# Chunked retention with a running state, run between the FFN matmuls, in a retention + FFN kernel

## The chip, the cores and the metric

The kernel runs on one core of one Trainium2 chip. The metric is the time of one execution on the device in microseconds (us), given as the median of several runs. Each kernel is also profiled once; the span of that profile (first to last instruction) is 1.7 to 2.8 us shorter than the time of the same execution. Engines are named as in the profile: PE is the matmul engine, PEld its weight loads, DVE the vector engine, ACT the scalar engine, POOL the general engine, SP the queue that issues most DMAs. PE writes its results to PSUM banks: in the changed kernel a bank is a tile of 128x512 f32 (`hp`, `st`, `op` and so on), which another engine must read before it is written again. An eviction is the copy out of a bank; a cast is a copy from f32 to f16.

## The reference

Retention is attention without softmax: scores are multiplied by a decay that depends on the distance between the two tokens, and future tokens are dropped. The result, laid out as 4608 tokens of 512 features, goes through an FFN with a tanh-approximated Gelu.

```python
# q, k, v: [8 batches, 8 heads, 576 tokens, 64]
scores = scale * q @ k.T
gamma  = 1.0 - 2.0 ** (-5.0 - arange(H))
ret    = scores * where(rel >= 0, gamma ** rel, 0.0)     # rel = i - j
attn   = ret @ v
x      = attn.transpose(0, 2, 1, 3).reshape(4608, 512)
h      = x @ w_in                                        # 512 -> 2048
g      = 0.5 * h * (1 + tanh(c * (h + 0.044715 * h**3)))
out    = g @ w_out                                       # 2048 -> 512
```

The FFN is nine blocks of 512 tokens; each needs 64 "up" and 64 "down" matmuls of 128x128 weights and 512 columns. The retention of one batch depends on nothing outside it, and FFN block t needs no batch beyond t.

## The kernel before

There are two stages in series. Stage one goes through 32 pairs of heads. Each pair is loaded in pieces of 64 floats, transposed in f32 on PE, and the full causal triangle of scores is masked on DVE:

```python
for b in range(B):
    for hp in range(HP):
        ...                                   # [cut: loads, v cast]
        qT = do_transpose(q2, "qT", scale)    # f32 transposes, ACT eviction
        kT = do_transpose(k2, "kT", 1.0)
        for J in range(NJ):                   # every key chunk ...
            w = S - 128 * J                   # ... against all later queries
            for (x0, n) in chunks:
                for hl in range(2):           # the two heads of the pair
                    nc.tensor.matmul(st, kT[...], qT[...], start=True, stop=True)
                for hl in range(2):
                    nc.vector.tensor_tensor(out=rets[hl][...], in0=sts[hl][...],
                                            in1=G[...], op=ALU.mult)
        ...                                   # [cut: AV matmuls, ACT evictions]
        nc.gpsimd.dma_start(out=xT[hp, :, b * S : (b + 1) * S], in_=xst)  # x to DRAM
```

Stage two reads x back and evaluates the Gelu in four steps, two on ACT and two on DVE, with four PSUM banks for `hps`:

```python
for tb in range(NTB):
    ...                                       # [cut: load xr from DRAM]
    for fc in range(16):
        hps = mps1.tile([128, TB], F32, ...)  # 4 banks
        ...                                   # [cut: 4 matmuls]
        nc.scalar.activation(out=s1, in_=hps, func=AF.Square, scale=SQ_SCALE)
        nc.vector.scalar_tensor_tensor(out=u, in0=s1, scalar=C_G, in1=hps, ...)
        nc.scalar.activation(out=th, in_=u, func=AF.Tanh)
        nc.vector.scalar_tensor_tensor(out=gT[:, fc, :], in0=th, scalar=1.0, in1=hps, ...)
    for tcc in range(4):
        ...                                   # [cut: 16 matmuls, eviction x 0.5, store]
```

## Time and profile before

| | before |
|---|---|
| time, median of 3 runs (range) | 539.69 us (534.5 to 547.18) |
| span of the profile | 536.7 us |
| retention, until the first FFN matmul | 277.9 us |
| FFN, nine blocks of 28.06 us and the tail | 258.8 us |

The first lines are from the page of the profile: busy time of each engine, then the same in 40 equal slices of the span, in tenths (the clock line shows what share of full speed PE was granted).

```profile
PE 458.3 (85%) x2432; PEld 232.2 (43%) x2432; DVE 317.3 (59%) x673; ACT 283.9 (53%) x527; POOL 23.7 (4%) x47
...
PE   0275699888888888888759999999999999999997
...
PEclk9999999889889899898659999999999999999999
DMA  8869646778776776720020202021111212020202
```

The 85% of PE is an average of two stages. The table of stretches separates them: the columns are the stretch, its length, the busy time of PE, PEld, DVE, ACT and POOL with instruction counts, the granted clock, the DMA share and GB/s.

```profile
100.00:200.00 100.00, 85.42 (x587) 50.80 (x586) 65.55 (x180) 38.08 (x89) 8.10 (x15) 0.93 0.73 161
355.06:383.12 28.06, 27.78 (x129) 12.50 (x128) 19.74 (x33) 20.11 (x36) 0.00 (x0) 1.00 0.17 57
```

The second line is one FFN block. PE works 27.78 of 28.06 us, and DVE and ACT have 8 us to spare: this stage is bound by PE. In the first line, retention, no engine is full. The view of waits (engine, line, what it waited for, total us, times, longest) says that DVE waits for the scores and PE waits for the masks (30.1 of DVE's 106.8 us is a single wait, at the start of the run):

```profile
DVE ret L176 <- PE st L167: 106.8, 36, 30.1
...
PE st L167 <- DVE ret L176: 27.0, 90, 0.8
```

These are groups of instructions (busy us and mean ns of one, then idle time before them):

```profile
L176 DVE TENSOR_TENSOR ret<-st,G 128x320 f16<-128x320 f32 (+5 forms) x384 | 139.3, 425 | 128.0 <-PE st L167 106.8
L229 PE MATMUL hps<-xr,w_in_sb 128*128 128x512 f16 x576 | 144.2, 382 | 8.5 <-DMA xr<-xT 5.6
...
L246 DVE SCALAR_TENSOR_TENSOR gT<-th,hps 128x512 f16<-128x512 f32 x144 | 97.5, 680 | 1.6 <-ACT th L245 0.7
```

A matmul record is longer than the matmul's share of the engine, because matmuls overlap in the pipeline: 382 ns here, while the starts of FFN matmuls are 216 ns apart. For PE, spacing is the number to use.

### The profile page before, as it was taken

To read this page: it belongs to the slowest core of one execution; us is meant where nothing else is said; L and a number is where in the kernel's file an instruction comes from. 1 tells how busy PE (TensorE), PEld (TensorE's weight loads), DVE (VectorE), ACT (ScalarE), POOL (GpSimd) and SP (SyncE) were. 2 spreads that over 40 slices of the span, in tenths; PEclk is the share of its full clock that TensorE was granted. 3 is DMA by queue.
4 is the path that set the end of the run, shared out by engine and by line. 5 is a ranking of instruction groups with operands and counts; after the bars stand their busy time and mean duration, and the time that the engine had idled before them with its cause. 6 is when DMAs were issued, how large, how long until landed. Compare 5 with 4: busy or idle time off the path is not lost.

```text
span 536.7 us, 7161 instructions
## 1 busy us (share of the span) xinstructions
PE 458.3 (85%) x2432; PEld 232.2 (43%) x2432; DVE 317.3 (59%) x673; ACT 283.9 (53%) x527; POOL 23.7 (4%) x47
## 2 busy tenths in 40 slices
PE   0275699888888888888759999999999999999997
PEld 0132255555545555454424444444444444444443
DVE  0033337566666666666519495867768594939392
ACT  0843535334333333343118585867777676858583
POOL 0300001000000000000000000000000000000000
PEclk9999999889889899898659999999999999999999
DMA  8869646778776776720020202021111212020202
GB/s 331 175 237 236 153 102 152 179 177 177 155 156 145 156 163 137 154 67 22 24 89 1 98 21 98 21 78 39 58 61 40 79 40 78 25 94 2 78 1 79
DMA packets 129733, 56.06 MB, mean 104 GB/s; under 512 B 116896, under 2 KB 121504, under 8 KB 129184
## 3 DMA queue, kind: packets, MB, share of 16 engines
q1 hardware_dynamic: 89760, 41.44, 28.6%
q10 hardware_dynamic: 38400, 9.44, 8.1%
q0 software_dynamic: 1536, 4.72, 2.9%
q8 instruction: 19, 0.31, 0.2%
q14 instruction: 18, 0.15, 0.1%
HBM read 41.42 MB, written 14.16 MB: 104 GB/s over the span
## 4 chain that ended last, share of the span: by engine, by line
PE 49%; issue 34%; DMA 6%; ACT 4%; DVE 3%; POOL 2%; ACTq 1%; SPq 0%; POOLq 0%; DVEq 0%
PE ops L257 23%; PE hps L229 20%; DMA wtmp_o<-in_moe_w_out_dram 3%; POOL xT L207 2%; PE trps L137 2%; DMA vh<-in_v_dram 2%; PE avA L188 2%; PE st L167 1%; ACT w_in_sb L84 1%; DVE gT L246 1%; DVE ret L176 1%; ACT G L62 1%; DVE u L241 1%; DMA xr<-xT 1%; PE avB L197 1%
## 5 line engine op out<-in xcount | busy, mean ns | idle before, releaser
L176 DVE TENSOR_TENSOR ret<-st,G 128x320 f16<-128x320 f32 (+5 forms) x384 | 139.3, 425 | 128.0 <-PE st L167 106.8
L229 PE MATMUL hps<-xr,w_in_sb 128*128 128x512 f16 x576 | 144.2, 382 | 8.5 <-DMA xr<-xT 5.6
L257 PE MATMUL ops<-w_out_sb,gT 128*128 128x512 f16 x576 | 141.3, 379 | 0.0
L246 DVE SCALAR_TENSOR_TENSOR gT<-th,hps 128x512 f16<-128x512 f32 x144 | 97.5, 680 | 1.6 <-ACT th L245 0.7
L167 PE MATMUL st<-qT,kT 64*128 64x320 f16 (+5 forms) x384 | 73.6, 298 | 27.5 <-DVE ret L176 27.0
L245 ACT ACTIVATE th<-u 128x512 f32<-128x512 f32 x144 | 89.4, 624 | 3.6 <-DVE u L241 3.1
L229 PEld LDWEIGHTS <-w_in_sb 128*128 128x128 f16 x576 | 56.5, 98 | 79.2 <-issue 13.5
L257 PEld LDWEIGHTS <-gT 128*128 128x128 f16 x576 | 56.3, 98 | 68.0
L143 ACT ACTIVATE qT<-trps 128x576 f16<-128x576 f32 x32 | 20.8, 650 | 89.1 <-PE st L167 64.3
L188 PE MATMUL avA<-ret,vr 128*64 128x512 f16 (+3 forms) x256 | 61.9, 379 | 2.1 <-DVE ret L176 0.2
L205 ACT CAST xst<-avA 128x512 f16<-128x512 f32 x32 | 18.7, 585 | 58.2 <-PE avA L188 37.7
L167 PEld LDWEIGHTS <-kT 64*128 64x128 f16 (+1 forms) x384 | 26.5, 98 | 52.7 <-issue 42.4
L265 ACT ACTIVATE ost<-ops 128x512 f32<-128x512 f32 x36 | 20.5, 596 | 50.6 <-PE ops L257 50.6
L188 PEld LDWEIGHTS <-vr 128*64 128x64 f16 x256 | 30.2, 130 | 31.8 <-issue 19.1
L197 PE MATMUL avB<-ret,vr 128*64 128x64 f16 (+1 forms) x320 | 32.6, 221 | 0.0
L197 PEld LDWEIGHTS <-vr 128*64 128x64 f16 (+1 forms) x320 | 26.5, 132 | 4.4
L207 POOL DMA_DIRECT2D xT<-xst x32 | 17.4, 544 | 232.9 <-ACT xst L206 232.9
L143 ACT ACTIVATE kT<-trps 128x576 f16<-128x576 f32 x32 | 20.7, 645 | 6.2 <-PE trps L137 4.6
L130 ACT CAST vr<-vh 128x512 f16<-128x512 f32 x32 | 20.2, 630 | 0.0
L137 PE MATMUL trps<-ident,q_104 128*128 128x128 f32 (+1 forms) x5 | 1.4, 414 | 17.6 <-DMA q_104<-in_q_dram 17.5
L131 ACT CAST vr<-vh 64x128 f16<-64x128 f32 x32 | 9.5, 298 | 0.0
L130 ACT ACT_TABLE_LOAD x1 | 1.3, 1283 | 14.9 <-DMA vh<-in_v_dram 14.9
(428 smaller groups left out, 330.4 us busy)
## 6 DMA issues: line engine op xcount, KB each, us to landing
out_dram<-ost SPq DMA_DIRECT2D x36, 256.0 KB, 2.0
vh<-in_v_dram ACTq DMA_DIRECT2D x64, 128.0 KB, 3.5
xT<-xst POOLq DMA_DIRECT2D x32, 144.0 KB, 2.3
xr<-xT SPq DMA_DIRECT2D x36, 128.0 KB, 2.4
wtmp_i<-in_moe_w_in_dram SPq DMA_DIRECT2D x1, 4096.0 KB, 13.4
wtmp_o<-in_moe_w_out_dram SPq DMA_DIRECT2D x1, 4096.0 KB, 15.9
vh<-in_v_dram ACTq DMA_DIRECT2D x32, 32.0 KB, 3.6
q_104<-in_q_dram SPq DMA_DIRECT2D x2, 128.0 KB, 2.2
```

Source lines behind the costliest of these rows:

```text
L130: nc.scalar.copy(out=vr[:, 0 : NJ - 1, :, :], in_=vh[:, 0 : NJ - 1, :, :])
L143: nc.scalar.activation(out=tsb, in_=ps, func=AF.Copy, bias=0.0, scale=sc_mul)
L167: nc.tensor.matmul(st[0:njs, 0:n], kT[poff : poff + 64, 128 * J : 128 * J + njs], qT[poff : poff + 64, 128 * J + x0 : 128 * J + x0 + n], s ...
L176: nc.vector.tensor_tensor(out=rets[hl][0:njs, J, x0 : x0 + n], in0=sts[hl][0:njs, 0:n], in1=G[0:njs, h0 + hl, x0 : x0 + n], op=ALU.mult,)
L188: nc.tensor.matmul(avA[poff : poff + 64, 128 * J : 512], vr[0:128, J, hl, :], ret[0:128, J, 0 : 512 - 128 * J], start=(J == 0), stop=(J == 3),
L197: nc.tensor.matmul(avB[poff : poff + 64, 0 : S - 512], vr[0:njs, J, hl, :], ret[0:njs, J, 512 - 128 * J : S - 128 * J], start=(J == 0), st ...
L207: nc.gpsimd.dma_start(out=xT[hp, :, b * S : (b + 1) * S], in_=xst,)
L229: nc.tensor.matmul(hps, w_in_sb[:, ct, 128 * fc : 128 * fc + 128], xr[:, ct, :], start=(ct == 0), stop=(ct == 3),)
L245: nc.scalar.activation(out=th, in_=u, func=AF.Tanh, bias=0.0, scale=1.0)
L246: nc.vector.scalar_tensor_tensor(out=gT[:, fc, :], in0=th, scalar=1.0, in1=hps, op0=ALU.add, op1=ALU.mult,)
L257: nc.tensor.matmul(ops, gT[:, ft, 128 * tcc : 128 * tcc + 128], w_out_sb[:, ft, :], start=(ft == 0), stop=(ft == 15),)
L265: nc.scalar.mul(out=ost, in_=ops, mul=0.5)
```

## The change

The intent is fourfold. Retention is done in 128-token chunks: inside a chunk by masked scores, across chunks by a 64x64 state per head that is carried on, so the work grows linearly with the length. The decay is put into q and k when they are cast to f16, so one 0/1 mask serves all heads. x stays in SBUF. The Gelu becomes one activation. And the order of PE is fixed by hand, so that the retention of batch t+1 runs in ten steps between the matmuls of FFN block t.

The core of the diff (heavily cut):

```diff
-  G = const.tile([128, H, S], F32, name="G")               # decay table per head
+  cm = const.tile([128, NC, 128], F32, name="cm")           # 0/1 causal mask of a chunk
-  xT = dram.tile([HP, 128, NT], F16, name="xT")
+  xT = const.tile([128, HP, NT], F16, name="xT")            # SBUF
+  def ld():                                                 # one ring for all f32 loads
+      return sb.tile([128, 512], F32, tag="ld", name="ld", bufs=15)
   ... [cut: load_batch, cast_batch (q or k times the decay), weight loads and casts]
+  def score_pairs(b, pairs, tail):      # 128x128 scores of each chunk, x cm on DVE
+  def state_mm(b):                      # k^T v of each chunk, 64x64, 32 matmuls
+  def state_scan(b):                    # DVE: w = gamma^128 (w + u); ACT copies to tbd
+  def av_pairs(b, pairs, tail):         # ret @ v, then += q @ state; ACT copies to xT
+  def up(fc):
+      hp = bank("hp", 2, "hp")                              # 2 banks, 6 for the rest
+      ... [4 matmuls]
+      nc.scalar.activation(out=gT[:, fc, :], in_=hp, func=AF.Gelu_apprx_tanh)
+  slots = {1: 0, 2: 1, 3: 2, 5: 3, 7: 4, 8: 5, 11: 6, 14: 7, 16: 8, 19: 9}
+  with tc.manual_schedule(engines={PE}):
+      load_batch(0); cast_batch(0, ...); [load w_in]; load_batch(1)
+      for s in att_steps(0): s()
+      [cast w_in; load and cast w_out]
+      for t in range(NTB):
+          if t + 1 < B: cast_batch(t + 1, ...); steps = att_steps(t + 1)
+          if t + 2 < B: load_batch(t + 2)
+          for i, f in enumerate(ffn_steps(t)):              # 16 up + 8 down steps
+              f()
+              if i in slots and slots[i] < len(steps): steps[slots[i]]()
```

## The prediction

> **What bounds the kernel now.** There are two stages in series. By the table of stretches and the chain of waits, retention lasts until 278 us and the FFN from there to 536.7 us.
> - FFN: each 512-token block of 128 matmuls takes 28.06 us (three equal stretches), PE busy 27.8 of it: 219 ns per 128x512 matmul. Nine blocks make 252.5 us. PE-bound.
> - Retention: about 6.5 us per head pair in steady state (timeline), 32 pairs. No engine is full: in 100–200 us PE is busy 85%, DVE 66%, DMA 73%; PE waits on the DVE mask (128x512: 686 ns) and DVE on PE.
> - Start: nothing but the w_in load until 17.5 us, then two 7 us weight casts blocking ACT.
>
> **What the change does.**
> - Removes quadratic scores: per batch the masked score columns drop from 8x1600 to 8x512+2x256, the f32 transposes (about 110 ns each at their spacing, 320 of them) become 36 f16 ones per batch, and the xT round trip through DRAM goes.
> - The FFN loses Square, Tanh and both DVE steps (ACT 20 and DVE 20 of 28 us per block); one Gelu of about 0.59 us remains. PE still needs 28.06 us per block. "ScalarE: Activation LUTs" (The pipeline for one element) says that every function costs the same per element; the trace's Square and Tanh (0.59, 0.62 us) agree.
> - PE order is fixed by hand: 156 small matmuls per batch (36 transposes, 36 scores, 32 state, 52 AV) go between FFN matmuls of the previous block.
>
> **Costing.** "TensorE: Matmul & The Clock Gate" (Back-to-back issue gap) gives about 81 ns per weight-load-plus-matmul at N=128. This trace's 64-column AV group issues every 72 ns; scores in two row halves overlap. Estimate 65 ns: 156 x 65 = 10 us per batch, seven times = 70 us in blocks 0 to 6.
> Estimated from the trace's durations, DVE needs 16–18 us per block (masks, scan, evictions, casts), ACT about 18, Pool about 10: below 38, so blocks are PE-bound. But with two hp banks (four before), fill 0.88 + drain 0.2 + Gelu 0.59 us just fits two periods of 0.88: the state copies on ACT, waiting for the scan on DVE, hold Gelus up. I allow 2 us per block, 14 us.
> Start: 18 q/k/v DMAs at about 0.6 us issue each, Pool casts of q and v, cold batch-0 retention: PE reaches the FFN near 33 us; then batch 1, whose loads wait for load buffers freed by the w_in casts, stalls it to about 47 us.
>
> **Sum.** 47 + 252.5 − 1.8 (two up steps done) + 70 + 14 + 3.5 (last eviction and store) = 385 us.
>
> **Prediction: 385 us, 80% range 360 to 410; faster 0.98, same 0.01, slower 0.01.**
>
> **What would show it right or wrong.** FFN matmuls stay at 219 ns spacing; blocks 7 and 8 take about 28 us each and blocks 0 to 6 about 40. Small matmuls cost 50–90 ns at their spacing. PE over 90% busy after 50 us, clock 1.0. One idle gap of about 10 us on PE at 33–47 us, released by casts of batch 1. A few PE waits per block on Gelu.
>
> **What would make it wrong.** Small matmuls at 90+ ns, or full row/column overlap (40 ns): ±25 us. Pool casts two to three times slower than about 1 us, through sharing with DVE, would stall every block. In-order ACT or DVE queues holding Gelu for microseconds. A smaller start-up if batch 1 arrives early.

(On the page "ScalarE: Activation LUTs" the sentence on equal cost stands under "Step-by-step: what each stage is for", not under the section that the prediction names. In the result below the Gelu takes 0.598 us, as long as Square and Tanh.)

## The result, and the profile after

| | before | after |
|---|---|---|
| time, median of 4 runs | 539.4 us | 361.74 us (360.63 to 361.88) |
| first FFN matmul | 277.9 us | 35.1 us |
| FFN block with a batch of retention inside | – | 35.1 to 35.9 us |
| FFN block alone | 28.06 us | 27.6 us |
| span | 536.7 us | 358.8 us |

The ratio of the times is 0.671 (95% interval 0.667 to 0.675).

The same lines of the page:

```profile
PE 316.4 (88%) x2400; PEld 159.1 (44%) x2400; DVE 125.9 (35%) x269; ACT 161.9 (45%) x303; POOL 70.3 (20%) x101
...
PE   0176368799999999999999999999999999999995
...
PEclk9995669899999999999999999999999999999999
DMA  9979989994692898598937931100110011011012
```

From the ninth slice on PE is full, to the last but one. The loads that used to keep the DMA engines busy in the retention stage are now spread over the first 60% of the run. The table of stretches, for batch 0's retention, the gap after it, one combined block, and one block without retention:

```profile
18.00:35.10 17.10, 10.92 (x146) 7.82 (x144) 14.23 (x31) 8.78 (x19) 1.34 (x3) 0.78 0.92 282
35.10:48.40 13.30, 4.56 (x18) 1.77 (x17) 2.77 (x4) 3.92 (x6) 6.00 (x7) 0.63 1.12 211
157.50:192.60 35.10, 34.54 (x285) 17.57 (x284) 14.99 (x29) 17.32 (x33) 10.30 (x15) 1.00 0.76 168
327.20:354.80 27.60, 27.60 (x129) 12.42 (x127) 0.00 (x0) 11.90 (x20) 0.00 (x0) 1.00 0.10 38
```

In the third line PE is busy 34.5 of 35.1 us and DVE and ACT about half of it, so the block is bound by PE. In the second, PE is busy for only 4.6 of 13.3 us while the DMA share is at its limit (the view can show a share slightly over 1). The groups that answer to those of before, and the waits of PE:

```profile
L355 PE MATMUL hp<-xT,w_in_sb 128*128 128x512 f16 x576 | 141.6, 388 | 7.7 <-ACT gT L361 7.5
...
L361 ACT ACTIVATE gT<-hp 128x512 f16<-128x512 f32 x144 | 85.2, 598 | 58.6 <-PE hp L355 57.9
...
L246 DVE TENSOR_TENSOR ret<-st,cm 128x512 f16<-128x512 f32 x64 | 40.7, 684 | 49.5 <-PE st L221 49.4
...
L246 DVE TENSOR_TENSOR rett<-st,tm 128x256 f16<-128x256 f32 x16 | 6.1, 413 | 0.0
```

```profile
PE tr L189 <- DVE ck L146: 15.0, 4, 5.7
PE tr L189 <- POOL ck L146: 8.5, 3, 3.5
PE hp L355 <- ACT gT L361: 7.5, 14, 1.9
```

The mask on DVE fell from 139.3 to 46.8 us (40.7 for the full chunks and 6.1 for the tails of 64 tokens). PE's waits are now few: 15 us for batch 0's first casts, 8.5 us for batch 1's, and 7.5 us in all for a Gelu to free an `hp` bank.

The small matmuls are the part that the prediction mis-sized. From the timeline of PE (start us, length us, instruction):

```profile
163.89 0.62 PE L221 MATMUL st<-qk 64*128 64x128 f16 x16
164.44 0.69 PE L258 MATMUL us<-cv,ck 128*64 128x64 f16 x32
```

Sixteen score matmuls take 164.44 − 163.89 = 0.55 us, 35 ns each with the hand-over; the single records, which this view merges and which were read from the packed trace, start in twos 3 ns apart, one two every 55 to 56 ns. The 32 state matmuls take 20 ns each, and eight full-array transposes take 0.45 us, 56 ns each. Over the six combined blocks after block 0, the starts of the small matmuls add up to 37.3 us: 6.2 us per batch, 40 ns per matmul.

### The profile page after: what moved, and what is told of

Its sections match the earlier page's. It is cut to its first block, busy times and chain, and to the rows that moved or that the text cites. A ratio compares the mean times of both kernels' runs of the same rounds, so it can differ in the third digit from the quotient of the medians.

```text
span 358.8 us, 6008 instructions
## 1 busy us (share of the span) xinstructions
PE 316.4 (88%) x2400; PEld 159.1 (44%) x2400; DVE 125.9 (35%) x269; ACT 161.9 (45%) x303; POOL 70.3 (20%) x101
## 2 busy tenths in 40 slices
DMA packets 122715, 46.52 MB, mean 130 GB/s; under 512 B 113984, under 2 KB 113984, under 8 KB 122688
## 3 DMA queue, kind: packets, MB, share of 16 engines
q1 hardware_dynamic: 122688, 46.15, 55.2%
## 4 chain that ended last, share of the span: by engine, by line
PE 67%; ACT 10%; DMA 9%; DVE 7%; SPq 4%; issue 1%; POOL 1%; DVEq 0%; ACTq 0%
PE op L369 35%; PE hp L355 24%; DVE ret L246 4%; ACT gT L361 4%; SPq L118 3%; DMA ld<-in_moe_w_out_dram 3%; DMA ld<-in_q_dram 3%; ACT tbd_128 L281 2%; ACT tbd_130 L281 2%; PE xs L290 2%; DMA ld<-in_moe_w_in_dram 2%; PE xs L308 2%; PE st L221 2%; PE tr L189 2%; DVE ws L278 1%; DMA ld<-in_v_dram 1%
## 5 line engine op out<-in xcount | busy, mean ns | idle before, releaser
L355 PE MATMUL hp<-xT,w_in_sb 128*128 128x512 f16 x576 | 141.6, 388 | 7.7 <-ACT gT L361 7.5
L369 PE MATMUL op<-w_out_sb,gT 128*128 128x512 f16 x576 | 128.1, 379 | 0.0
L361 ACT ACTIVATE gT<-hp 128x512 f16<-128x512 f32 x144 | 85.2, 598 | 58.6 <-PE hp L355 57.9
L369 PEld LDWEIGHTS <-gT 128*128 128x128 f16 x576 | 55.6, 98 | 65.3
L377 ACT COPY ost<-op 128x512 f32<-128x512 f32 x36 | 21.1, 586 | 100.9 <-PE op L369 66.0
L246 DVE TENSOR_TENSOR ret<-st,cm 128x512 f16<-128x512 f32 x64 | 40.7, 684 | 49.5 <-PE st L221 49.4
L146 POOL TENSOR_TENSOR ck<-ld,sc 128x512 f16<-128x512 f32 (+1 forms) x35 | 34.8, 997 | 82.2 <-DMA ld<-in_k_dram 60.9
L195 DVE COPY qk<-tr 128x1024 f16<-128x1024 f16 x32 | 21.9, 686 | 56.5 <-PE tr L189 56.5
L146 DVE TENSOR_TENSOR cq<-ld,sc 128x512 f16<-128x512 f32 (+1 forms) x35 | 22.6, 660 | 40.2 <-DMA ld<-in_q_dram 40.2
L142 POOL CAST cv<-ld 128x512 f16<-128x512 f32 (+1 forms) x40 | 23.1, 590 | 67.4 <-DMA ld<-in_v_dram 36.8
L281 ACT CAST tbd_128<-ws 64x256 f16<-64x256 f32 x32 | 12.9, 403 | 3.1 <-DVE ws L278 2.6
L281 ACT CAST tbd_130<-ws 64x256 f16<-64x256 f32 x32 | 12.9, 403 | 2.4 <-DVE ws L278 2.0
L221 PE MATMUL st<-qk 64*128 64x128 f16 x256 | 11.9, 226 | 0.3 <-DVE qk L195 0.3
```

What stands on the lines that cost most here:

```text
L142: eng[key].tensor_copy(out=dst, in_=raw)
L146: eng[key].tensor_tensor(out=dst.rearrange("p (h d) -> p h d", d=D), in0=raw.rearrange("p (h d) -> p h d", d=D), in1=sc[:, s0 : s0 + nh].u ...
L195: nc.vector.tensor_copy(out=s, in_=t)
L221: nc.tensor.matmul(st[hl][:, 128 * c : 128 * c + 128], qk[r, 128 * c : 128 * c + 128], qk[r, 512 + 128 * c : 512 + 128 * c + 128], start=T ...
L246: nc.vector.tensor_tensor(out=r, in0=st[:, 0:w], in1=m.rearrange("p c i -> p (c i)"), op=ALU.mult)
L281: nc.scalar.copy(out=td[r, c, :, r], in_=w[r])
```

## The experiments

Times are medians of four runs. The changed kernel at 361.74 us is the reference for all edits of it; it and the kernels close to it scatter by under 1%, and the kernel before by about 1% between chips (539.4 to 545.7 us, medians with the slow runs in them). The changed kernel was not run again beside the experiments, so a difference of a few us is taken seriously only where the block times of the traces show it too.

| run | edit | time us | ratio to before |
|---|---|---|---|
| e1_gelu_only | before + one Gelu activation | 533.16 | 0.988 |
| e2_four_op_gelu | after + the old four-step Gelu | 534.84 | 0.992 |
| e12_four_op_four_hp | e2 with four `hp` banks | 452.43 | 0.839 |
| e3_stages_apart | after, all retention first | 441.56 | 0.819 |
| e10_apart_wide | e3, loads in 2 KB rows (wrong result) | 413.46 | 0.765 |
| e4_halves_apart | after, head loop outermost | 363.56 | 0.675 |
| e9_one_row_half | after, all scores on one row half (wrong result) | 365.94 | 0.678 |
| e5_more_load_bufs | after, 19 load buffers for 15 | 360.61 | 0.664 |
| e6_wide_rows | after, loads in 2 KB rows (wrong result) | 353.01 | 0.650 |
| e7_batch1_last | after, batch 1 loaded after w_out | 350.95 | 0.647 |
| e8_three_hp | after, three `hp` banks | 356.90 | 0.657 |
| e11_best | e7 and e8 together | 349.75 | 0.648 |

### What the single Gelu is worth, and where

```diff
 # e1, in the kernel before
-  Square on ACT; scalar_tensor_tensor on DVE; Tanh on ACT; scalar_tensor_tensor on DVE
+  nc.scalar.activation(out=gT[:, fc, :], in_=hps, func=AF.Gelu_apprx_tanh)
-  nc.scalar.mul(out=ost, in_=ops, mul=0.5)
+  nc.scalar.copy(out=ost, in_=ops)
```

> The kernel before with only its Gelu changed: one Gelu activation in place of Square, DVE, Tanh, DVE. Theory (the FFN is bound by PE, 27.8 of 28.06 us per block busy): ACT falls from 20 to about 12 us and DVE from 20 to 0 us per block, and the time falls by at most 9 x 0.43 = 4 us, to 530-540 us, class same. Rival (the four-step Gelu was what held the FFN back): faster by more than 5%.

Measured: 533.16 us, ratio 0.988 (0.982 to 0.993). Only its FFN stretch at full clock is used:

```profile
343.39:371.02 27.63, 27.63 (x129) 12.54 (x128) 0.00 (x0) 11.89 (x20) 0.00 (x0) 1.00 0.17 58
```

DVE falls from 19.7 to 0 and ACT from 20.1 to 11.9 us, and the block from 28.06 to 27.63. The rival is out: work was taken from engines that were not the limit. Nine blocks at 0.43 us make 3.9 of the 6 us; the rest lies within the scatter of the kernel before.

```diff
 # e2, in the changed kernel (two hp banks); one ost and one qk buffer fewer for room
-  nc.scalar.activation(out=gT[:, fc, :], in_=hp, func=AF.Gelu_apprx_tanh)
+  Square on ACT; scalar_tensor_tensor on DVE; Tanh on ACT; scalar_tensor_tensor on DVE
```

> The changed kernel with the old four-step Gelu put back on its two hp banks (one load buffer fewer for ost and qk to make room). Theory (latency of a bank): fill 0.86 + drain 0.2 + 0.59 + 0.69 + 0.62 + 0.68 + hand-overs is about 3.7 us for a bank, two banks, so an up step takes about 1.8 us in place of 0.86: blocks 7 and 8 take about 43 us each, blocks 0 to 6 about 46, the time is 440-500 us. Rival (throughput only: DVE 16 + 20 = 36 us per block against PE 35): 370-385 us.

Measured: 534.84 us, worse than the range. The throughput rival (370 to 385) is clearly out. An FFN block without retention takes 48.9 us, and its 16 up steps 2.19 us each, where 1.8 was expected:

```profile
429.43:478.35 48.92, 34.89 (x129) 13.85 (x128) 21.28 (x32) 21.12 (x36) 0.00 (x0) 0.83 0.06 22
```

No engine is full, and the granted clock of 0.83 is probably part of the miss: the block is 21 us longer than one of 27.6 us, PE's waits for a bank make 14.0 of them (seven waits of 2.0 us), and the other 7 would be matmuls at the lower clock. "TensorE: Matmul & The Clock Gate" (The HAM clock gate) of the Trainium skill says that PE is throttled to half speed by default and after an idle window of about 3.4 us, and that activity releases it. The trace agrees in that a PE that is busy for less of the time gets less clock: 0.83 here, and 0.63 at 35 to 48 us in the changed kernel, where it is busy for a third. No single wait in this block is as long as that window, and the clock was not tested by itself.

```diff
 # e12, on top of e2 (two qk and two ret buffers fewer in all, for room)
-  hp = bank("hp", 2, "hp");  bank("att", 6, ...);  g: bufs=2
+  hp = bank("hp", 4, "hp");  bank("att", 4, ...);  g: bufs=4
```

> The four-step Gelu in the changed kernel again, now with four hp banks and four shared ones, as many hp banks as the kernel before had. Theory (with two banks the latency of a bank's chain, 2.19 us per up step, was what cost 173 us, not the throughput of DVE or ACT): blocks 7 and 8 fall from 49 us to 34-39 us (DVE's two steps, 1.37 us per up step, bound the up phase then), time 420-465 us. Rival (throughput of the in-order ACT and DVE queues): blocks 7 and 8 stay above 45 us, time over 500 us.

Measured: 452.43 us, inside the range. PE's waits for a bank, by the view of waits, first of e2 and then of e12:

```profile
PE hp L355 <- DVE gT L370: 127.5, 83, 4.5
```

```profile
PE hp L355 <- DVE gT L370: 26.6, 44, 3.3
PE us L258 <- DVE ret L246: 23.9, 15, 2.8
```

A block without retention is back at 32.0 us (a little below the expected 34 to 39). So of e2's 173 us, 82 go with the two more banks: the wait on the bank's chain, and the lower clock that came with it. That is a net figure, since e12 also has two shared banks fewer and two more `g` buffers. The other 91 stay even with four: the blocks with retention take 47.6 us in place of 35.4, with new waits on the four shared banks, and DVE and ACT then carry both the Gelu and the retention. By block, 73 of the 91 us lie in blocks 1 to 6; how they split by cause was not tested. What is shown is that one activation is worth 6 us in the kernel before and 91 us or more in the changed one, which without it would still beat the kernel before (452 us), but by half as much.

### What the interleaving is worth

```diff
 # e3: the loop over FFN blocks no longer calls retention steps
+  for b in range(1, B):
+      cast_batch(b, ...); load_batch(b + 1)
+      for s in att_steps(b): s()
   for t in range(NTB):
-      [FFN steps with retention steps of batch t+1 in the slots]
+      for f in ffn_steps(t): f()
```

> The changed kernel, all instructions kept, but all eight batches of retention run before the first FFN block. Theory (the interleaving hides retention's loads, casts and DVE chain behind FFN matmuls): retention alone is bound by DMA or by its DVE chain at 14-18 us per batch though PE needs 6, so the FFN starts near 150 us and the time is 385-420 us; FFN blocks take 27.6 us each. Rival (the gain is only the smaller work on PE, interleaving adds nothing): 365 us or less.

Measured: 441.56 us. The direction is as expected and the size larger: the FFN starts at 185.1 us, not near 150. The 178 us between the two kernels split here: 98 us come with chunked retention, the single Gelu and x in SBUF, still in two stages; 80 us come from the interleaving. The 14 to 18 us per batch were nearly right: a batch is 3.5 MB (3 x 8 heads x 576 x 64 x 4 bytes), and in this trace the last loads of batches 2 to 7 land 18.2 us apart. What the expectation left out is the weights: w_in and w_out are 8.4 MB more, and they take about 29 us of the same DMA engines, between batches 0, 1 and 2. This is the view of a stretch of q, k and v loads alone:

```profile
100.00:160.00 60.00, 43.17 (x552) 31.48 (x549) 49.66 (x92) 18.02 (x42) 25.68 (x32) 0.57 1.07 199
```

199 GB/s at a share of 1.07, while the granted clock of PE is 0.57. To see whether DMA alone sets this, the same kernel was run with wide rows:

```diff
 # e10 (and e6): same bytes and same number of DMAs, but wrong tokens and heads
-  in_=src[b, :, 128*c : 128*c+128, :].rearrange("h s d -> s h d")          # 256-byte pieces
+  in_=src[b].rearrange("h (s w) d -> (h s) (w d)", w=8)[128*c : 128*c+128, :]   # 2 KB rows
```

> Wrong result on purpose: the stages-apart kernel with q, k and v loaded in 2 KB rows in place of 256-byte pieces. Theory (with the stages apart, retention's 185 us are bound by DMA: share 0.9 to 1.0, 36.7 MB at about 200 GB/s): the FFN starts at 120-145 us, time 375-400 us. Rival (bound by the chain of PE, DVE and ACT within a batch): the FFN starts at 170 us or later, time over 425 us.

Measured: 413.46 us; the FFN starts at 156 us. This lies between the two theories. The rate rises to 302 GB/s and the share falls below 1:

```profile
40.00:100.00 60.00, 39.28 (x534) 29.73 (x534) 52.68 (x99) 21.93 (x48) 32.36 (x39) 0.61 0.89 302
```

DVE is now busy 52.7 of 60 us. So 256-byte pieces cost 29 of e3's 185 us, and under them DVE is nearly as tight a limit (its q casts are longer in this run too, 957 ns for 839, so part of its load comes from the edit). Either way, interleaving hides it: in the changed kernel these loads and DVE work lie behind FFN matmuls.

### Why the small matmuls were cheaper than predicted

```diff
 # e4: head loop outermost in scores, state and AV (same matmuls, other order)
-  for c in range(NC):
-      for hl in range(2):
+  for hl in range(2):
+      for c in range(NC):
```

> The changed kernel with the loop over the two heads of a pair outermost in scores, state and AV, so neighbouring matmuls use the same half of the array in place of alternate halves; same work. Theory (alternate halves overlap in the array: 29 ns spacing for scores and AV, 20 for state, against 54 for full-array transposes): spacing rises to about 54 ns, 104 matmuls x 25 ns = 2.6 us per batch, the time rises by 15-23 us to 376-386 us. Rival (half-array matmuls are simply that cheap, order does not matter): within 3 us of 362.

Measured: 363.56 us, against an expected 376 to 386. By the clause on record this speaks for the rival. The timeline of e4 shows which parts moved:

```profile
165.15 0.64 PE L221 MATMUL st<-qk 64*128 64x128 f16 x16
165.71 1.10 PE L258 MATMUL us<-cv,ck 128*64 128x64 f16 x32
```

Scores stay at 35 ns (0.56 us for 16). The state matmuls, which now come in runs of 16 on the same half, went from 0.63 to 1.03 us: 2.4 us over six blocks, more than the whole rise of 1.8 us. So for them the order did matter. The single records of e4's scores start 13 and 43 ns apart in turn, so two streams still run side by side although the program has four matmuls of one half in a row. For the scores, the experiment had not taken the overlap away. A stronger one does: all scores read the same row half.

```diff
 # e9: head 0 used twice, wrong result
-  r = slice(64 * hl, 64 * hl + 64)
+  r = slice(0, 64)
```

> Wrong result on purpose: the changed kernel, but all score matmuls of a pair read rows 0 to 63 of q and k (head 0 twice), so no score matmul can run beside one on the other row half; same count and sizes. Theory (two half-array matmuls run at once; the trace of the changed kernel starts score matmuls in twos 3 ns apart every 53-56 ns; the earlier reordering kept the overlap because each half's run was only four long): scores start one by one every 54 ns, 36 x 27 ns = 1 us per batch, time up by 6-9 us to 367-371 us. Rival (a half-contraction matmul is simply half as long): spacing stays 28-35 ns, within 2 us of 362.

Measured: 365.94 us, up 4.2 us, less than the 6 to 9 expected, but the spacing is as the theory has it:

```profile
165.67 1.06 PE L221 MATMUL st<-qk 64*128 64x128 f16 x16
166.66 0.69 PE L258 MATMUL us<-cv,ck 128*64 128x64 f16 x32
```

Sixteen scores now take 0.99 us, and the single records start one by one every 55 to 57 ns. So two matmuls on different row halves do run at once, and one of them alone is not cheaper than a full one (56 ns for a transpose of 128 columns). Part of the rise is taken back by fewer waits for Gelu (over six blocks the FFN part shrinks by 1.0 us and PE's waits for Gelu fall from 4.6 to 3.5; the small matmuls grow by 5.3 us).

### The start

```diff
 # e5 (two qk, two ret, one ost buffer fewer for room)
-  tag="ld", bufs=15
+  tag="ld", bufs=19
```

> The changed kernel with 19 load buffers in place of 15 (room made by two fewer qk, two fewer ret and one fewer ost buffer). Theory (the DMA engines are saturated up to 66 us, share 0.92 to 1.08): within 2 us of 362. Rival (as predicted: batch 1's loads wait for load buffers to be freed): the gap before batch 1's transposes shrinks by about the issue time of four loads, 4 us or more, time 358 us or less.

Measured: 360.61 us, within the 2 us, and PE's wait for batch 1's casts is unchanged:

```profile
PE tr L189 <- POOL ck L146: 8.3, 3, 3.4
```

Four more load buffers did not shorten the gap, nor did batch 1's first load go out earlier: it was issued at 30.0 us, after 29.6 in the changed kernel. The prediction's reason for it, loads that wait for buffers, is not supported.

> Wrong result on purpose: the changed kernel, but q, k and v tiles are loaded as rows of 512 consecutive floats (2 KB) in place of eight pieces of 64 floats (256 B); same bytes, same number of DMAs, same everything else. Theory (256-byte pieces saturate the DMA engines in the start-up): packets fall from 122,700 to below 40,000, a batch's loads take well under half the time, the FFN starts near 25 us in place of 35, the gap at 38-48 us mostly closes, and the time is 335-348 us. Rival (issue of DMAs and the Pool casts set the start): 355-362 us.

Measured: 353.01 us, with the edit shown at e10 and a wrong result. It falls just under the rival's range and well short of 335 to 348. Packets fell as expected (page of e6):

```profile
DMA packets 27483, 46.52 MB, mean 133 GB/s; under 512 B 3392, under 2 KB 6464, under 8 KB 27456
```

The profile after has 122,715 packets. The gap before batch 1's transposes shrinks: PE waits 1.7 us for POOL in place of 8.5, and block 0 ends at 75.0 us in place of 86.9. So the gap was DMA. But the first FFN matmul only moves from 35.1 to 32.1 us, because batch 0's own chain of casts, masks, scan and copies takes most of that time (its last load lands at 13.6 us, and its last AV matmuls run up to 32.1), and blocks 1 to 4 take 36.3 to 36.7 us in place of about 35.4, with more waits for Gelu (9.5 us in place of 7.5). DVE's q casts also got longer in e6, from 720 to 966 ns; why was not tested.

```diff
 # e7
   for g in range(4): load_w_in(g)
-  load_batch(1)
   ...
   for f in range(NF): cast_w_out(f)
+  load_batch(1)
   ...
+  late = {18: (0, 1), 19: (2, 3), 20: (4, 5), 21: (6,), 22: (7, 8), 23: (9,)}   # block 0
```

> The changed kernel with batch 1 loaded after w_out in place of before it, and batch 1's retention steps moved to the last six half-steps of FFN block 0. Theory (start-up is bound by the order in which DMA delivers: batch 0, w_in, batch 1, w_out in 61 us; block 0's up phase needs only the first two): no gap at 38-48 us, block 0 ends near 75-78 us in place of 87, time 347-356 us. Rival (the gap only moves to w_out or to the end of block 0): within 3 us of 362.

Measured: 350.95 us, correct. Block 0's 64 up matmuls and its first 24 down matmuls run with only short waits, while w_out and batch 1 arrive (timeline of PE):

```profile
52.30 5.34 PE L369 MATMUL op<-w_out_sb,gT 128*128 128x512 f16 x24
57.48 0.33 PE L189 MATMUL tr<-ident,ck 128*128 128x128 f16 x3
58.89 0.23 PE L189 MATMUL tr<-ident,ck 128*128 128x128 f16 x1 [1.09 <-POOL ck L146]
```

Block 0 ends at 75.3 us, 11.6 us earlier. The bytes and the work are the same; what changed is the order of delivery and, to fit it, the place of batch 1's steps. This is the version to keep: it beats both kernels.

```diff
 # e8
-  bank("hp", 2, "hp");  bank("att", 6, ...)
+  bank("hp", 3, "hp");  bank("att", 5, ...)
```

> The changed kernel with three hp banks in place of two, and five shared banks for the rest in place of six. Theory (in-order ACT holds Gelus behind the state copies, PE waits 0.6-0.8 us per block for a bank): PE's waits on Gelu go from 7.5 us to under 1, time 354-360 us. Rival (fewer shared banks give new waits on evictions that eat it): 360-370 us.

Measured: 356.90 us. In the six combined blocks the changed kernel's PE waits for Gelu 4.6 us; e8 has, in the same blocks:

```profile
PE us L258 <- DVE ret L246: 1.1, 6, 0.2
PE hp L355 <- ACT gT L361: 0.6, 1, 0.6
```

Both theories hold a part: the wait on Gelu nearly goes, and a small wait on the five shared banks comes.

> Batch 1 loaded last (late steps in block 0) together with three hp banks and five shared ones; correct result. If the two gains add: 351 - 5 = 343-348 us; if they share a cause: 349-352 us.

Measured: 349.75 us, correct, ratio 0.6476 against 0.6469 for e7 in another set of rounds. The gains do not add; the 1 us between e7 and e11 is not clear of the scatter. The traces show where: blocks 1 to 6 do gain (210.3 us in place of e7's 214.0), but block 0 takes 41.6 us in place of 39.8.

## Why the prediction was right or wrong

The time was inside the range (385, 360 to 410), near its fast end. The trace allows the sum to be checked term by term (us):

| term | predicted | measured in the trace |
|---|---|---|
| up to the end of block 0 | 47 − 1.8 + 40.1 = 85.3 | 86.9 |
| blocks 1 to 6 | 6 x 40.1 = 240.4 | 212.7 |
| blocks 7 and 8 | 56.1 | 55.2 |
| last eviction and store | 3.5 | 4.0 |
| sum | 385 | 358.8 (span) |

The first row agrees partly by luck. After the gap, block 0 still took 38.5 us; a later block, without the two up steps that were done before the gap, would have taken about 33.7 (35.4 − 1.7, an estimate). That slower stretch, with 3.0 us of waits for Gelu and a clock of 0.89 up to 66 us, made up for the small matmuls that were put too high.

- **The FFN is bound by PE: right.** e1 shows it before the change, the blocks of 27.6 us after it.
- **Steady blocks are bound by PE: right.** DVE was put at 16 to 18 us per block, ACT at 18 and Pool at 10; measured 15.0, 17.3 and 10.3.
- **The mis-sized term: "Estimate 65 ns: 156 x 65 = 10 us per batch".** Measured: 40 ns, 6.2 us. This is 3.8 of the 4.6 us by which a block was over-estimated; the rest is 27.6 for 28.06 and 1.6 us of waits and hand-overs for 2. The figure of 81 ns that the estimate leaned on does not describe this kernel: full-array matmuls of 128 columns start every 56 ns, and matmuls on two halves overlap. The prediction knew of the overlap ("scores in two row halves overlap") and gave it too little weight; it even named "full row/column overlap (40 ns)" as what would take 25 us off, and that is what was measured.
- **The gap at 33 to 47 us: right in place and size** (35.1 to 48.4 us), **wrong in its reason.** The prediction blamed load buffers freed by the w_in casts; e5 speaks against that, and e6 and e7 show that it was the order and speed of DMA delivery. That batch 0 reaches the FFN near 33 us was right too (35.1), and e6 shows that DMA is only a small part of it.
- **Two `hp` banks just fit: right.** The wait exists (0.8 us per block, 7.5 us in all) and e8 takes it away.
- **Not foreseen:** how much the change depends on the single Gelu (e2). The prediction read it as removed work that leaves PE's 28.06 us per block as they are, which is nearly true of the kernel before (e1) and not of the changed one.
- **Left open:** how e3's 98 us divide among the chunked scores, the f16 transposes and x in SBUF; what fixing the order of PE by hand is worth by itself; and how e2's remaining 91 us split.

## What to carry to other kernels

Work that is bound by loads and by a chain of dependent steps costs little when it is cut into short pieces and placed between dense matmuls of something else; here that alone is worth 80 us of 441. Taking work from an engine that is not the limit changes little by itself, but it can be what makes such a placement pay, so a part that is worth 1% alone may be worth far more in the whole (here 91 us or more). At the start, ask in which order the bytes are needed: the same loads in another order saved 11 us.

## What the Trainium skill lacked or had wrong

- "TensorE: Matmul & The Clock Gate" (Back-to-back issue gap) gives a sustained 81 ns per weight-load-plus-matmul at N=128 and 131 ns at N=512, and calls the isolated formula of 56 and 216 ns an under- and an over-count. Here the sustained spacing is 55 to 57 ns at 128 columns (transposes; scores of e9) and 216 ns at 512: the isolated formula is right for this kernel. So are the back-to-back gaps of 55.6 and 215.7 ns that the same page measured elsewhere (Part 1), against its own roofline.
- The same page (Packing small matmuls, The mechanism) says that matmuls start and end strictly in program order. In e4, with four same-half matmuls in a row in the program, scores start 13 and 43 ns apart in turn, while e9 shows 55 to 57 ns for matmuls on the same half. So a matmul on the other half starts ahead of its turn. The records agree: the matmul that ends a head's score tile updates a semaphore; in each eight of e4's score matmuls these are the fourth and the eighth of the program, but the seventh and the eighth to start. Runs of 16 in the state matmuls lose the overlap (20 to 32 ns each).
- The same page (PE-mode transpose) gives about 275 ns for a 128x128 transpose within a kernel. The records here are about 220 ns long, but eight f16 transposes pass in 0.45 us, 56 ns each; no throughput is given.
- "DMA: Bandwidth & Descriptors" (Specifications) says that transfers below 512 bytes are not at line rate, with no rate in GB/s for them (under "Why small descriptors are slow" it puts the overhead of a 256-byte descriptor at 27%). Here a stream of 256-byte pieces ran at 199 GB/s with the DMA engines full (e3), and 2 KB rows of the same bytes at 302 GB/s with a share of 0.89 (e10).
